# Zero rows between the queries' heads: written from a tile on chip, in two parts, instead of from a row in DRAM

## The chip, the cores and the metric

The kernel runs on one core of a Trainium2 chip. The core has a matrix engine (TensorE, PE in the profile; its weight loads are PEld), a vector engine (VectorE, DVE), a scalar engine (ScalarE, ACT), a general engine (GpSimd, POOL) and a sync engine (SyncE, SP), which here does little but issue transfers. Each engine works through its own list of instructions in order, and semaphores hold an engine until another engine, or a transfer, is done. Sixteen DMA engines move data between DRAM and the memories on chip. The metric is the device time of one execution in microseconds (us).

## The reference

The inputs are x (2048 rows of 640), and the weights of an attention with 32 heads of 20 and of a two-layer network with 1536 hidden units. Both act on 2048 rows, and a gate mixes their outputs row by row.

```python
x = A_x
g = sigmoid((x * gate_w).sum(-1, keepdims=True))
# a: attention
qkv = (x @ wqkv).reshape(B, S, 3, H, Dh).transpose(2, 0, 3, 1, 4)     # H = 32, Dh = 20
p = softmax(einsum("bhqd,bhkd->bhqk", q, k) * Dh ** -0.5)
a = einsum("bhqk,bhkd->bhqd", p, v).transpose(0, 2, 1, 3).reshape(B, S, D) @ wo
# b: network
h = einsum("bsd,df->bsf", B_x, w1) + b1
act = h * tanh(softplus(h))
b = einsum("bsf,fd->bsd", act, w2)
out = g * a + (1 - g) * b
```

## The kernel before

Heads are worked on in eight groups of four, queries in four blocks of 512. For each group and block the scores stand with the keys on the partitions: sixteen key tiles of 128 by 512 queries, for each of the four heads. A head has 20 rows, and matmuls on a quarter of the array take 32, so in the tiles QT (queries) and KT (keys) each head has 32 rows of which 12 are padding. The padding of QT must be zero.

ScalarE takes most of the exponentials: it reads two or three score tiles of 128x512 in one instruction from PSUM and writes bf16 to a ring (L1166, tile ETS). The score matmuls are L1139, the matmuls with the values L1375. VectorE takes over 118 of the 512 groups of four tiles: it makes an integer line of each tile (L1224), and shifted copies of it (L1254) which, read as float16 and weighted (VS, made by POOL at L1279), add up to the exponential. PE gives each pair of PSUM slots back when ACT has read it.

When a group is done its sums go through small transfers: VectorE copies the accumulator to OUNG (L1462), SP moves the sums to RR (L1465), VectorE inverts them (L1469), SP writes them to DRAM (SUMS<-RR, L1470) and reads them back spread over the partitions (BCT<-SUMS, L1472), and VectorE multiplies (L1432). All of this stands in the same lists as the rest.

x is needed with its columns on the partitions, in four blocks of 512 rows (XB). Block 0 is loaded as rows (L491) and transposed by PE; blocks 1 to 3 come by transposing transfers on SP (L497). Queries and keys of group 0 are made by L563 from padded weights: five matmuls for each block of x. The other groups' keys and queries are made unpadded, in denser matmuls (L625, L644 and L672), and spread by way of DRAM. For the queries, VectorE copies six heads' rows to a tile in WOQ (L680), SP writes them to the DRAM tensor QS with 32 rows for each head (QS<-WOQ, L683), and later SP reads 128 rows of QS back to QT (QT<-QS, L699). QS holds 28 heads (those of groups 1 to 7) for each of the four query blocks. The 12 rows between two heads are written once, by one transfer for each block: `clear(c)`, L593, QS<-ZEROS. Its source is one row of 512 zeros in the DRAM tensor ZEROS, repeated 336 times; ZEROS itself is written by a POOL transfer at the start. The keys take the same way through KS (L601, L617, KS<-ZEROS at L587), with ZEROS as the source of a few rows behind the last head. Every QS<-WOQ of a block waits for `q_blank[c]`, the transfer of zeros of that block.

The network's hidden units go to the tile HB (L917 adds the bias, L941 and three VectorE operations make the activation, L967 multiplies by the second weights). HB is first written at 195.73 us, apart from a second part of it which VectorE's lines use.

The order of all this is written by a planner when the program is built. It goes step by step, one ScalarE exponential to each step, keeps a modelled time for each engine, and at each step chooses from the open tasks (each with a due step) by a table of some sixty numbers: costs, margins and due steps. `later(step, fn)` puts an action at a fixed step. A new number changes the order wherever a choice was close; no number changes what is computed. At the end the last group is normalized on VectorE alone (L1447 to L1455), the output matmuls (L991) follow, and VectorE mixes their results with the network's (L997) into HB, from where they go out (L1023). A second plan, for inputs beyond a bound, stands behind a branch and is not run.

Of the kernel before, what the change touches and what calls it, by code (L numbers as in the profile page):

```python
# [21 lines left out]
H = 32  # L22
DH = 20
NG = 8
HG = 4
# [3 lines left out]
NC = 4  # L29
CW = 512  # L30
# [26 lines left out]
WIDE = 0.60  # L57
# [3 lines left out]
BLOCK = 0.43  # L61
STEP = 1.1
SLACK = 0.191
LATER = 0.79
THIRD = 0.425
CALLED = 0.978
ROWED = 3
SPARED = 0
KEPT = 8
NEED = 5  # L70
BEFORE = 4
FREE = 0.242
RISK = {"pe": 0.1, "act": 0.3, "dve": 0.5, "pool": 1.2, "sp": 1.2}
AHEAD = 17
BEHIND = 23.3
MORE = 5.902
PATIENCE = 5.499
CATCH_UP = 497.751
BUSY = 0.437
CROWD = 1.459  # L80
MARGIN = 0.679
EAGER = 121
LOAD = 1.134
MISH = 1.7
GROUP = 1.526
LAST = 0
# [1 line left out]
XSLACK = 0.468  # L88
BROAD = 1.13
FMIN = 0.109  # L90
VMIN = 12.188
ROOM = 1.319
TURN = 1
MORE_MM = 0.005
XBANKS = 2
# [1 line left out]
BEND = -0.18501488  # L97
QUART = (-1.86851238, -11.55859586, -2.86851238)
LEAD = 0.0214693053
END = 61  # L100
SHIFT = 1.385
LAG = 343
WINDOW = 2.785
CALM = 10
PACKED = 17
Q_AT = 120
# [129 lines left out]
def bass_gated_mix__softmax_full_mha__dense_activation_mish__prompt_kernel(  # L236
# [34 lines left out]
    HB = sb("HB", [P, 2, NFC, HW], BF16)  # L271
# [18 lines left out]
    QS = nc.dram_tensor("QS", [NC, 32 * (H - HG), CW], BF16, kind="Internal")  # L290
# [69 lines left out]
    def attention(pl, fast):  # L360
# [54 lines left out]
        def later(step, fn):  # L415
            at.setdefault(step, []).append(fn)
# [60 lines left out]
        b1f = []  # L477
# [3 lines left out]
        if fast:  # L481
# [13 lines left out]
            def load_x(c):  # L495
                xt_load[c] = [pl.add(
                    "sp", lambda e: e.dma_start_transpose(xt(c), x_ap[c * CW:(c + 1) * CW, :]), (), f"xt{c}", cost=4.5)]  # L497
# [14 lines left out]
            blank = early[0:NG, 4 * D + P:5 * D + P]  # L512
            m_blank = pl.add("dve", lambda e: e.memset(blank, 0.0), cost=0.25)
            m_mxs = pl.add("dve", lambda e: e.memset(MXS[:, :], 0.0))
            m_bias = pl.add("dve", lambda e: e.memset(MXR[:, 3:4], BEND))

            for i in range(10):
                pl.add("pe", lambda e: e.matmul(
                    PS[:, 5, :], RING[:, 0, 0:P], RING[:, 0, :], start=True, stop=True),
                    [m_zero] if i == 0 else [], cost=2 * PASS)  # L520
            load_x(1)
            load_x(2)

            def wbulk(name, dst, src):
# [32 lines left out]
            def kq_task(k, g, c, due, forced=True):  # L557
# [28 lines left out]
            none = ZEROS.ap()[:, 0:CW]  # L586
            k_blank = [pl.add("sp", lambda e, c=c: e.dma_start(  # L587
                KS.ap()[c, D:D + 12, :], none.to_broadcast([12, CW])), [zeros], "kz", cost=0.5) for c in range(NC)]

            def clear(c):  # L590

                to = QS.ap()[c, :, :].rearrange("(h r) t -> h r t", r=32)[:, DH:32, :]
                return pl.add("sp", lambda e: e.dma_start(to, bass.AP(  # L593
                    tensor=none.tensor, offset=none.offset, ap=[[0, H - HG], [0, 32 - DH], [1, CW]])), [zeros], f"qz{c}", cost=0.5, bulk=0.5)

            q_blank = [clear(c) for c in range(NC)]

            def shelve(name, c, rows, src, ev, n, i=0):

# [220 lines left out]
            guarded = []  # L820
# [78 lines left out]
            def h_task(hc, k, due):  # L899
# [11 lines left out]
                def finish(bank, last):  # L911
                    x_read[c].append(last)
                    w1_last[n1] = last
                    if n1 + 2 < FIRST or FIRST <= n1 < 6 * NHC - 2:
                        load_w1(n1 + 2)
                    bias = B1F[:, 2 * k:2 * k + 2].unsqueeze(2).to_broadcast([P, 2, HW])
                    ev = dve(lambda e: e.tensor_tensor(  # L917
                        hb, PS[:, bank, :].rearrange("p (i t) -> p i t", i=2), bias, ALU.add),
                        [last, *b1f, *guarded, *b_read.get(hc - 2, []), *(line_free[("h", 0)] if hc == 1 else ())], WIDE)
                    if k % 2:  # L920
                        both = HB[:, part, 2 * k - 2:2 * k + 2, :]
                        acts.append((ev, lambda: mish(ev, both, hc, k)))
                    return ev
# [556 lines left out]
        if fast:  # L1480
# [35 lines left out]
            tasks.extend(gram_task(n, SQ + SQ_STEP * n) for n in range(8))  # L1516
            tasks.extend(h_task(hc, k, H_AT + int(H_STEP * (6 * hc + k))) for hc in range(2) for k in range(6))
            tasks.sort(key=lambda t: t.due)
            later(H_AT - 90, lambda: (load_w1(0), load_w1(1)))
            rest = []  # L1520

# [157 lines left out]
        while True:  # L1679
# [50 lines left out]
            while owed > 0:  # L1730
                t = pick(limit)
# [182 lines left out]
```

## Time and profile before

| | |
|---|---|
| median of 3 runs | 781.88 us (781.61 to 783.07) |
| the profiled execution | 784.62 us |
| its span, from the first to the last instruction | 782.8 us |
| mean granted TensorE clock | 0.989 |
| busy: PE / DVE / ACT / POOL | 747.7 / 684.8 / 752.6 / 149.9 us |
| transfers of zeros to QS | 4, of 336 KB each, issued from 24.93 us on |

Times in the profile count from the start of the span. In a row of the timeline stand the start, the time it lasts, the engine (SPq is SP's issuing of transfers), the line, the operation with output <- input, the count, and in brackets the idle time ahead of it with what ended it. In a row of a group stand the count, the busy time and the mean ns of one, and then the idle time of the engine just before. In a row of the chain stand the start, the time and the work. In a row of stretches there are the busy times of PE, PEld, DVE, ACT and POOL with the number of instructions, then PE's granted clock, DMA's busy time and the GB/s that the DMA engines moved. "DMA to landing" counts from the issue. In a row of waits stand the total, the number of waits and the longest.

### The profile page before, as it was taken

Reading aid. Unit: us, or ns where it says so; the run is one execution under the profiler, and the core shown is the slowest. Engines: PE = TensorE matmul, PEld = TensorE weight load, DVE = VectorE, ACT = ScalarE, POOL = GpSimd, SP = SyncE. Lnnn points to the kernel's source line nnn. Section 1 sums busy time; section 2 is a strip of 40 time slices with the busy share of each in tenths; the row PEclk is TensorE's granted clock in tenths of the full one; section 3 lists DMA queues with packets and bytes.
Section 4 is the critical chain, followed back from the end, with each engine's and each line's share of the span. In section 5 each row is a group of like instructions: output and inputs, shape, how many; then the busy total and the mean of one; then the engine's idle time right before and its main releaser. Section 6 shows DMA issues by size and latency. Waiting matters only on the chain.

```text
span 782.8 us, 17174 instructions
## 1 busy us (share of the span) xinstructions
PE 747.7 (96%) x7176; PEld 273.9 (35%) x7176; DVE 684.8 (87%) x1108; ACT 752.6 (96%) x797; POOL 149.9 (19%) x258
## 2 busy tenths in 40 slices
PE   8969999999999999989999999999999999999996
PEld 3323334333332343223333333333333333333332
DVE  3558998999998899977798989998999999999786
ACT  5959999999999999999999999999999999999995
POOL 3203115102232013212211111311112121203200
PEclk9979999999999999999999999999999999999998
DMA  9541321021223430361111122201222211100001
GB/s 229 77 74 53 94 73 33 15 75 47 71 72 102 119 93 24 82 172 42 50 56 49 52 65 66 66 23 34 59 71 59 70 52 56 46 20 20 27 14 46
DMA packets 77804, 49.89 MB, mean 64 GB/s; under 512 B 21232, under 2 KB 73704, under 8 KB 77672
## 3 DMA queue, kind: packets, MB, share of 16 engines
q1 hardware_dynamic: 75352, 48.24, 23.2%
q8 instruction: 59, 0.97, 0.6%
q10 hardware_dynamic: 2256, 0.47, 0.3%
q0 software_dynamic: 112, 0.01, 0.1%
q14 instruction: 25, 0.20, 0.1%
HBM read 39.01 MB, written 8.90 MB: 61 GB/s over the span
## 4 chain that ended last, share of the span: by engine, by line
ACT 69%; PE 20%; DMA 6%; DVE 4%; issue 0%; SPq 0%
ACT ETS L1166 66%; PE PS L1139 7%; PE PS L1375 6%; ACT REG L941 2%; DMA W2R<-in_B_w_dram 2%; PE PS L625 2%; DMA QS<-WOQ 2%; PE PS L672 1%; PE PS L789 1%; PE PS L907 1%; DMA SUMS<-RR 1%; PE PS L830 1%; PE PS L762 1%; DMA BCT<-SUMS 1%; ACT W2R L941 1%; DMA LN<-in_A_x_dram 1%
## 5 line engine op out<-in xcount | busy, mean ns | idle before, releaser
L1166 ACT ACTIVATE ETS<-PS 128x1024 bf16<-128x1024 f32 (+1 forms) x766 | 729.1, 1134 | 14.1 <-PE PS L1139 12.6
L1139 PE MATMUL PS<-QT,KT 32*128 32x512 bf16 (+1 forms) x2118 | 300.2, 379 | 19.0 <-ACT ETS L1166 16.0
L1224 DVE TENSOR_SCALAR LN<-PS 128x512 int16<-128x512 f32 x364 | 245.1, 683 | 25.4 <-PE PS L1139 23.1
L1279 POOL TENSOR_SCALAR VS<-V_all 128x84 bf16<-128x84 bf16 x244 | 142.6, 584 | 589.3 <-PE PS L1375 396.5
L1139 PEld LDWEIGHTS PS<-QT,KT 32*128 32x128 bf16 x2118 | 74.3, 91 | 242.5 <-ACT ETS L1166 218.9
L1375 PE MATMUL PS<-ETS,V_all 128*21 128x512 bf16 (+1 forms) x1624 | 150.0, 377 | 0.3 <-DVE V_all L770 0.3
L1254 DVE TENSOR_SCALAR LN<-LN 128x2048 int16<-128x2048 int16 x163 | 111.0, 687 | 12.2 <-PE PS L1375 11.7
L967 PE MATMUL PS<-W2R,HB 128*128 128x320 bf16 x384 | 74.0, 302 | 0.5 <-DMA W2R<-in_B_w_dram 0.5
L1375 PE MATMUL PS<-LN,VS 128*21 128x512 f16 (+1 forms) x768 | 70.5, 377 | 0.0
L907 PE MATMUL PS<-XB,REG 128*128 128x256 bf16 x360 | 58.1, 275 | 0.3 <-DVE LN L1224 0.2
L1375 PEld LDWEIGHTS PS<-ETS,V_all 128*21 128x21 bf16 x1624 | 38.6, 91 | 52.8 <-issue 36.7
L991 PE MATMUL PS<-WOQ,QT 128*128 128x320 bf16 x256 | 50.9, 303 | 0.9 <-DVE QT L1455 0.9
L967 PEld LDWEIGHTS PS<-W2R,HB 128*128 128x128 bf16 x384 | 29.9, 97 | 34.8 <-issue 25.1
L1224 DVE TENSOR_SCALAR REG<-PS 128x512 int16<-128x512 f32 x52 | 34.6, 678 | 6.1 <-PE PS L1139 6.0
L907 PEld LDWEIGHTS PS<-XB,REG 128*128 128x128 bf16 x360 | 28.8, 97 | 26.3 <-issue 24.0
L1375 PE MATMUL PS<-LN,V_all 128*21 128x512 f16 (+1 forms) x380 | 35.6, 373 | 0.0
L917 DVE TENSOR_TENSOR HB<-PS,B1F 128x512 bf16<-128x512 f32 x48 | 32.6, 680 | 1.5 <-PE PS L907 1.3
L672 PE MATMUL PS<-XB,WOQ 128*120 128x512 bf16 (+1 forms) x100 | 31.4, 399 | 0.3 <-DVE WOQ L680 0.3
L991 PEld LDWEIGHTS PS<-WOQ,QT 128*128 128x128 bf16 x256 | 19.7, 97 | 25.5 <-issue 17.6
L1375 PEld LDWEIGHTS PS<-LN,VS 128*21 128x21 bf16 x768 | 17.4, 89 | 27.7 <-issue 18.8
L1462 DVE COPY OUNG<-PS 128x512 f32<-128x512 f32 x31 | 21.3, 686 | 5.6 <-PE PS L1375 5.4
L789 PE MATMUL PS<-REG,XB 128*128 128x160 bf16 (+1 forms) x240 | 25.3, 234 | 0.0
(128 smaller groups left out, 553.6 us busy)
## 6 DMA issues: line engine op xcount, KB each, us to landing
REG<-in_B_w_dram SPq DMA_DIRECT2D x36, 320.0 KB, 3.2
BCT<-SUMS SPq DMA_DIRECT2D x31, 256.0 KB
W2R<-in_B_w_dram SPq DMA_DIRECT2D x12, 320.0 KB, 4.0
QT<-QS SPq DMA_DIRECT2D x28, 128.0 KB, 2.3
KT<-KS SPq DMA_DIRECT2D x28, 128.0 KB
KS<-LN SPq DMA_DIRECT2D x16, 128.0 KB, 3.4
QS<-WOQ SPq DMA_DIRECT2D x16, 120.0 KB
W2R<-in_B_w_dram SPq DMA_DIRECT2D x1, 1920.0 KB, 13.8
```

The costliest lines, as they stand in the source:

```text
L672: return lambda e, bank: e.matmul(PS[0:m, bank, :], WQ[:, f, base:base + m], xt(c)[:, f, :], start=(f == 0), stop=(f == NFT - 1))
L789: return lambda e, bank: e.matmul(PS[:, bank, i * n:(i + 1) * n], xt(t // 4)[:, f, t % 4 * P:(t % 4 + 1) * P], WV[:, f, g * HD:g * HD + n] ...
L907: return lambda e, bank: e.matmul(PS[:, bank, i * HW:(i + 1) * HW], w1b(n1)[:, f, i * P:(i + 1) * P], xt(c)[:, f, cols], start=(f == 0), s ...
L917: ev = dve(lambda e: e.tensor_tensor(hb, PS[:, bank, :].rearrange("p (i t) -> p i t", i=2), bias, ALU.add), [last, *b1f, *guarded, *b_read ...
L967: return lambda e, bank: e.matmul(PS[:, bank, 0:HALF], HB[:, hc % 2, f, t * P:(t + 1) * P], W2[:, f, half * HALF:(half + 1) * HALF], start ...
L991: return lambda e, bank: e.matmul(PS[:, bank, 0:HALF], otn(c, g)[:, t * P:(t + 1) * P], WOG[:, g, half * HALF:(half + 1) * HALF], start=(g ...
L1139: op = pl.add("pe", lambda e, to=to, g=real(g), tile=tile, j=j, cols=cols, c=c, of_q=of_q: e.matmul(to[:, cols], KT[32 * j:32 * j + 32, g, ...
L1166: e_op[s] = pl.add("act", lambda e: e.activation(RING[:, p:p + n, :], scores(s)[:, 0:n, :], AF.Exp, scale=SCALE), [s_op[s], *(pv_slot[b] f ...
L1224: bank_free[bank] = x_ops[bank] = tile["op"] = dve(lambda e: e.tensor_scalar(dst, PS[:, bank, :], SCALE * ULPS, BASE, ALU.mult, ALU.add), ...
L1254: op = pl.add("dve", lambda e: e.tensor_scalar(to, src, SHADES[n] - SHADES[held], None, ALU.add), [made, *deps], cost=SHADE)
L1279: weighted[(c, g, k)] = n, [pl.add("pool", lambda e, i=i, n=n, src=src: e.tensor_scalar(VS[:, n, i, :, :], src, WEIGHTS[i + 1], None, ALU. ...
L1375: lasts[n] = pl.add("pe", lambda e, v=v, j=j, src=src[:, cols], of_q=of_q, begin=begin, end=end: e.matmul(PS[32 * j:32 * j + EW, ACC, of_q ...
```

## The change

The zeros' source becomes a part of HB: 28 partitions with 512 zeros each, which VectorE sets near the start (`none_q`). Each of the 28 partitions is read twelve times for the twelve rows of its head. The transfers of blocks 0 and 1 are issued between the transposing loads of x's blocks 1 and 2; those of blocks 2 and 3 go out at fixed steps, 80 and 100. They no longer wait for ZEROS but for the memset. The first writes of HB by the network wait for all four. Ten of the planner's numbers are set anew, of which two are shown.

```diff
-LATER = 0.79
+LATER = 1.264
...
-END = 61
+END = 65
...
             m_mxs = pl.add("dve", lambda e: e.memset(MXS[:, :], 0.0))
+            none_q = HB[0:H - HG, 0, 0:2, :].rearrange("p f t -> p (f t)")
+            m_none = pl.add("dve", lambda e: e.memset(none_q, 0.0), cost=0.3)
             m_bias = pl.add("dve", lambda e: e.memset(MXR[:, 3:4], BEND))
...
             load_x(1)
+            q_blank = {}
+
+            def clear(c):
+
+                to = QS.ap()[c, :, :].rearrange("(h r) t -> h r t", r=32)[:, DH:32, :]
+                q_blank[c] = pl.add("sp", lambda e: e.dma_start(
+                    to, none_q.unsqueeze(1).to_broadcast([H - HG, 32 - DH, CW])), [m_none], f"qz{c}", cost=0.8, bulk=2.5)
+
+            clear(0)
+            clear(1)
             load_x(2)
...
-            def clear(c):
-
-                to = QS.ap()[c, :, :].rearrange("(h r) t -> h r t", r=32)[:, DH:32, :]
-                return pl.add("sp", lambda e: e.dma_start(to, bass.AP(
-                    tensor=none.tensor, offset=none.offset, ap=[[0, H - HG], [0, 32 - DH], [1, CW]])), [zeros], f"qz{c}", cost=0.5, bulk=0.5)
-
-            q_blank = [clear(c) for c in range(NC)]
...
-                        [last, *b1f, *guarded, *b_read.get(hc - 2, []), *(line_free[("h", 0)] if hc == 1 else ())], WIDE)
+                        [last, *b1f, *guarded, *b_read.get(hc - 2, q_blank.values()), *(line_free[("h", 0)] if hc == 1 else ())], WIDE)
...
+            later(Q_AT - 40, lambda: clear(2))
+            later(Q_AT - 20, lambda: clear(3))
```

Lines behind the change move by 4 to 12 numbers. On SP, the start of the program before (LN are x's first rows, XB its transposed blocks, REG and WOQ the weights):

```order
L491 DMA LN<-in_A_x_dram 128x2x640 x2
L497 DMA_TRANSPOSE XB<-in_A_x_dram 128x5x512 x2
L525 DMA REG<-in_A_wqkv_dram 128x5x560
L525 DMA WOQ<-in_A_wqkv_dram 128x5x560
L525 DMA REG<-in_A_wqkv_dram 128x5x560
L497 DMA_TRANSPOSE XB<-in_A_x_dram 128x5x512
L587 DMA KS<-ZEROS 12x512 x4
L593 DMA QS<-ZEROS 28x12x512 x4
L683 DMA QS<-WOQ 6x20x512
```

and now:

```order
L491 DMA LN<-in_A_x_dram 128x2x640 x2
L497 DMA_TRANSPOSE XB<-in_A_x_dram 128x5x512
L529 DMA QS<-HB 28x12x512 x2
L497 DMA_TRANSPOSE XB<-in_A_x_dram 128x5x512
L537 DMA REG<-in_A_wqkv_dram 128x5x560
L537 DMA WOQ<-in_A_wqkv_dram 128x5x560
L537 DMA REG<-in_A_wqkv_dram 128x5x560
L497 DMA_TRANSPOSE XB<-in_A_x_dram 128x5x512
L599 DMA KS<-ZEROS 12x512 x4
L687 DMA QS<-WOQ 6x20x512
```

Two of the four transfers have moved past two loads of x, the three weight loads and the four small KS<-ZEROS; none is left ahead of the first QS<-WOQ. The third stands further down on SP, now, among the reads of keys (KT<-KS) of the second pass:

```order
L1469 DMA RR<-OUNG 128x1x16
L605 DMA KS<-LN 128x512
L621 DMA KT<-KS 128x1x512 x2
L529 DMA QS<-HB 28x12x512
L621 DMA KT<-KS 128x1x512 x2
L1474 DMA SUMS<-RR 128x16
L1476 DMA BCT<-SUMS 128x1x512
```

where before four KT<-KS stood together, directly ahead of SUMS<-RR. On DVE the multiplication that waits for this BCT (L1432) stood before in this place:

```order
L1224 TENSOR_SCALAR HB<-PS 128x512 x2
L1254 TENSOR_SCALAR LN<-LN 128x2048
L1432 TENSOR_TENSOR QT<-OUNG,BCT 128x512
L1224 TENSOR_SCALAR HB<-PS 128x512
L680 CAST WOQ<-PS 128x512
L1224 TENSOR_SCALAR LN<-PS 128x512 x3
```

and now:

```order
L1228 TENSOR_SCALAR HB<-PS 128x512 x2
L1258 TENSOR_SCALAR LN<-LN 128x2048
L1228 TENSOR_SCALAR HB<-PS 128x512
L684 CAST WOQ<-PS 128x512
L1228 TENSOR_SCALAR LN<-PS 128x512
L1436 TENSOR_TENSOR QT<-OUNG,BCT 128x512
L1228 TENSOR_SCALAR LN<-PS 128x512 x2
```

Three operations have moved ahead of it. At the end of DVE's list, before (W2R and HB are the mixes' outputs):

```order
L997 SCALAR_TENSOR_TENSOR HB<-PS,GATE,W2R 128x320
L1254 TENSOR_SCALAR LN<-LN 128x2048
L997 SCALAR_TENSOR_TENSOR HB<-PS,GATE,W2R 128x320 x3
L1449 STREAM_TRANSPOSE BCT<-PS 128x256
L1450 RECIPROCAL RR<-BCT 128x8
L1451 STREAM_TRANSPOSE BCT<-RR 128x256
L1455 TENSOR_TENSOR QT<-PS,BCT 128x256
L997 SCALAR_TENSOR_TENSOR HB<-PS,GATE,W2R 128x320 x3
```

and now:

```order
L1258 TENSOR_SCALAR LN<-LN 128x2048 x2
L1001 SCALAR_TENSOR_TENSOR W2R<-PS,GATE,XB 128x320 x2
L1453 STREAM_TRANSPOSE BCT<-PS 128x256
L1454 RECIPROCAL RR<-BCT 128x8
L1455 STREAM_TRANSPOSE BCT<-RR 128x256
L1459 TENSOR_TENSOR QT<-PS,BCT 128x256
L1001 SCALAR_TENSOR_TENSOR W2R<-PS,GATE,XB 128x320
L1001 SCALAR_TENSOR_TENSOR HB<-PS,GATE,W2R 128x320 x7
```

Five of the mixes have moved behind the last normalization. On PE, fourteen output matmuls (L995) stand in one piece between the last attention matmuls and the final eight, where before there was none. Over the whole list ACT has 740 exponentials of 1024 columns and 32 of 1536, where it had 722 and 44; the number of VectorE's lines is the same.

More of the change, by code (lines that the diff above doesn't have):

```diff
@@ L69 @@
 KEPT = 8
-NEED = 5
+NEED = 4
 BEFORE = 4
-FREE = 0.242
+FREE = 0.278
 RISK = {"pe": 0.1, "act": 0.3, "dve": 0.5, "pool": 1.2, "sp": 1.2}
-AHEAD = 17
+AHEAD = 18
 BEHIND = 23.3
@@ L79 @@
 BUSY = 0.437
-CROWD = 1.459
+CROWD = 1.561
 MARGIN = 0.679
 EAGER = 121
-LOAD = 1.134
+LOAD = 0.794
 MISH = 1.7
@@ L90 @@
 FMIN = 0.109
-VMIN = 12.188
-ROOM = 1.319
+VMIN = 11.335
+ROOM = 0.923
 TURN = 1
@@ L99 @@
 LEAD = 0.0214693053
-END = 61
+END = 65
 SHIFT = 1.385
 LAG = 343
-WINDOW = 2.785
+WINDOW = 2.367
 CALM = 10
```

## The prediction

> **What bounds the kernel now.** I read the page first: the engines' busy shares, the chain that ended last, and the groups of instructions.
>
> ```profile
> PE 747.7 (96%) x7176; PEld 273.9 (35%) x7176; DVE 684.8 (87%) x1108; ACT 752.6 (96%) x797; POOL 149.9 (19%) x258
> ACT 69%; PE 20%; DMA 6%; DVE 4%; issue 0%; SPq 0%
> L1166 ACT ACTIVATE ETS<-PS 128x1024 bf16<-128x1024 f32 (+1 forms) x766 | 729.1, 1134 | 14.1 <-PE PS L1139 12.6
> ```
>
> ScalarE's exponentials (L1166) are 729.1 of the 782.8 us and 69% of the chain. They wait only 14.1 us in all, 12.6 of it for score matmuls (L1139). So the end moves with three things: how much ACT has to do, where ACT stands idle, and what follows its last exponential. The second question is where those 14.1 us are. The waits of ACT between 46 and 62 us give the first row below; the timelines of ACT, PE and DVE show the hole itself.
>
> ```profile
> ACT ETS L1166 <- PE PS L1139: 9.8, 6, 6.6
> 53.64 1.02 ACT L1166 ACTIVATE ETS<-PS 128x1024 bf16<-128x1024 f32 x1 [6.56 <-PE PS L1139]
> 52.50 0.56 PE L762 MATMUL PS<-REG,XB 128*128 128x80 bf16 x6 [6.32 <-DVE HB L1224]
> 51.56 0.25 DVE L1469 RECIPROCAL RR<-RR 128x16 f32<-128x16 f32 x1 [6.88 <-DMA RR<-OUNG]
> ```
>
> 9.8 of the 14.1 us lie in one place, and the largest piece, 6.56, is a queue of waits: ACT for PE, PE for DVE, DVE for the little transfer RR<-OUNG, which carries the softmax sums. That transfer is quick, so I ask what it stood behind: SP's timeline, the chain between 28 and 60 us, and, for comparison, the same pair of transfers in a quiet stretch.
>
> ```profile
> 24.93 5.70 SPq L593 DMA_DIRECT2D QS<-ZEROS  x4
> 36.24 0.73 SPq L683 DMA_DIRECT2D QS<-WOQ  x1
> 49.22 0.34 SPq L699 DMA_DIRECT2D QT<-QS  x1
> 49.60 0.60 SPq L1465 DMA_DIRECT2D RR<-OUNG  x1
> ...
> 36.24 12.97 DMA QS<-WOQ
> 49.60 1.93 DMA RR<-OUNG
> ...
> 186.66 0.77 SPq L683 DMA_DIRECT2D QS<-WOQ  x1
> 189.52 0.33 SPq L699 DMA_DIRECT2D QT<-QS  x1
> ```
>
> The first transfer of query rows (QS<-WOQ) needs 12.97 us; in the quiet stretch its reader follows 2.86 us after it. It went out behind the four transfers of zeros, QS<-ZEROS. SP then sits at QT<-QS until 49.22, and RR<-OUNG is next on SP. The stretches of time say how slowly the zeros move, and what the hole does to TensorE's clock (the column before the last two).
>
> ```profile
> 16.00:20.00 4.00, 4.00 (x42) 1.65 (x40) 1.18 (x2) 4.00 (x5) 0.20 (x1) 1.00 1.50 352
> 26.00:36.00 10.00, 9.92 (x92) 3.50 (x91) 6.14 (x10) 10.00 (x12) 3.01 (x8) 1.00 0.46 64
> 36.00:48.00 12.00, 10.18 (x87) 2.58 (x79) 8.68 (x15) 11.08 (x13) 0.00 (x0) 1.00 0.70 74
> ...
> 46.00:48.00 2.00, 0.18 (x1) 0.00 (x0) 0.00 (x0) 1.08 (x2) 0.00 (x0) 1.00 0.46 85
> 48.00:61.70 13.70, 9.20 (x70) 2.75 (x70) 6.89 (x12) 5.12 (x5) 1.91 (x5) 0.50 0.25 78
> ```
>
> While weights load, the DMA engines move 352 GB/s; from 26 to 48 us, with the zeros in their queues, 64 to 74. Four blocks of 336 rows of 1 KB are 1.38 MB, at some 65 GB/s 21 us: from 26 to about 47, just when QS<-WOQ is at last served. The clock is 0.50 from 48 to 61.7, and that is why five small gaps of ACT follow: 9.8 - 6.56 = 3.2 us.
>
> **The change part by part.** *The hole.*
>
> ```profile
> 40.38 0.68 DVE L1462 COPY OUNG<-PS 128x512 f32<-128x512 f32 x1
> ```
>
> The four slow transfers no longer stand ahead of the first QS<-WOQ: two are moved to the start of SP's program, two behind it, and none reads the row in DRAM. QS<-WOQ should land in about 2.9 us, near 40; RR<-OUNG then goes out when its data are there (41.1 by this row), lands 1.93 later, and the reciprocal, which DVE reached at 44.7 (51.56 - 6.88), finds it. What is late next: nothing that I find, since DVE's next matmul inputs come at once after it. PE does not stop, so the clock stays and the five gaps go too: -9.8 us. The bounds are -6.56 (the gaps stay) and -9.8.
>
> *The start.* Two issues now stand between the transposing loads of x's blocks 1 and 2. Behind them come block 2, three weight loads and block 3.
>
> ```profile
> 1.74 8.53 SPq L497 DMA_TRANSPOSE XB<-in_A_x_dram  x2
> 12.08 9.67 SPq L497 DMA_TRANSPOSE XB<-in_A_x_dram  x1
> DMA to landing us min/median/max: 11.6/11.6/11.6
> 18.53 0.38 PE L563 MATMUL PS<-XB,REG 128*128 128x512 bf16 x1
> 23.87 0.38 PE L563 MATMUL PS<-XB,REG 128*128 128x512 bf16 x1
> 24.22 0.09 PEld L1139 LDWEIGHTS PS<-QT,KT 32*128 32x128 bf16 x2 [0.28 <-ACT ETS L1166]
> L593 SPq DMA_DIRECT2D QS<-ZEROS x4: 750/776/3267, 24.9 to 27.4; - x4
> ```
>
> Block 3 is issued at 12.08 and lands 11.6 later (the third row is of that issue alone), at 23.7. Its first use is the key matmul at 23.87 (block 2's is the one at 18.53; block 2 was out of SP by 10.3, so it has time to spare). So whatever is put ahead of block 3 delays it, and PE, which works in order, then stops ahead of the scores at 24.22. Those had 0.28 us in hand, so ACT loses the delay less about 0.4. The delay: SP issues, 2 x 0.776 = 1.55, are the lower end if the queues have room; the data, 2 x 0.344 MB, take 2.0 us at 352 GB/s and 10.6 at 65. A write from the chip is in no way tied to the one DRAM row that all old zeros were read from, so I take the fast side, 1.8 us: 1.4 us of ACT. Ends: 0 (the queues had gaps) and 10.2.
>
> Here the Trainium skill speaks against the change: in "SBUF — State Buffer", section "Door 1: The DMA port swizzle", a transfer's rate goes by the ports that its partitions reach, 27.2 GB/s each. By that table partitions 0 to 27 reach seven ports, 190 GB/s, an estimate of 3.6 us for the two blocks; the loss would be 3.2 us and the sum 1.8 higher. No row of this trace shows a wide write from 28 partitions.
>
> *The memset* that makes the zeros stands on DVE ahead of its 3.36 us of waiting for the first transposes (first row below): nothing. *The later two writes.* One goes out among the four KT<-KS, ahead of the sums' way back, near 100 us.
>
> ```profile
> 6.49 2.10 DVE L711 CAST XB<-PS 128x512 bf16<-128x512 f32 x3 [3.36 <-PE PS L726]
> ...
> 100.70 6.04 DMA SUMS<-RR
> 112.18 0.69 DVE L1432 TENSOR_TENSOR QT<-OUNG,BCT 128x512 bf16<-128x512 f32 x1 [0.90 <-DMA BCT<-SUMS]
> 195.73 0.68 DVE L917 TENSOR_TENSOR HB<-PS,B1F 128x512 bf16<-128x512 f32 x1
> ```
>
> The sums' transfer already took 6.04 us there and DVE waited 0.90 for its end. One more block adds 0.78 of issue and 1.0 us of data at 352 GB/s, 1.8 together; but the new order lets DVE do three more operations of 0.6 to 0.7 us ahead of L1432. I put it at nothing, with ends -0.4 and +5 (5.3 us of data at 65 GB/s, less what DVE does meanwhile). That the first bias adds into HB (L917) now wait for all four writes costs nothing: the first is at 195.73, some 80 us behind the last write's place.
>
> *ACT's work.* Twelve exponentials of 1536 columns become eighteen of 1024; the columns are the same, and so are the 118 tiles that DVE takes over.
>
> ```profile
> L1166 ACT ACTIVATE ETS<-PS 128x1024 bf16<-128x1024 f32 x722 | 680.1, 1107 | 14.1 <-PE PS L1139 12.6 <-PE PS L1375 1.4
> L1166 ACT ACTIVATE ETS<-PS 128x1536 bf16<-128x1536 f32 x44 | 69.2, 1584 | 0.0
> ```
>
> 512 columns are 1584 - 1107 = 477 ns, so an instruction carries 153 ns of its own; six more are at most 0.9 us. Successive ones overlap (722 x 1107 is 799, busy 680), so I take 0.4, ends 0 and 0.9.
>
> *The tail.*
>
> ```profile
> 775.08 0.71 PE L991 MATMUL PS<-WOQ,QT 128*128 128x320 bf16 x4
> 776.17 0.42 DVE L1455 TENSOR_TENSOR QT<-PS,BCT 128x256 bf16<-128x256 f32 x1
> 777.14 1.47 DVE L997 SCALAR_TENSOR_TENSOR HB<-PS,GATE,W2R 128x320 bf16<-128x320 f32 x3 [0.54 <-PE PS L991]
> ```
>
> Before, only three of DVE's final mixes (L997) come after the last normalization (L1455); in the new order eight do, and PE has fourteen output matmuls left behind its last attention matmul. Five more mixes at 0.46 (1.47 for three, overlapping) are 2.3 us, less the 0.54 that DVE waited, less some 0.3 because fewer attention matmuls are left when ACT ends: about +1.5, ends 0.5 and 2.3.
>
> *The rest of the order* changes from about 125 us on, by retuned numbers. The gaps of ACT outside the hole are 14.1 - 9.8 = 4.3 us; I have no row for the new ones and take the same, ends -3 and +4.
>
> *Sum:* -9.8 + 1.4 + 0 + 0.4 + 1.5 = -6.5 us. The profiled execution, 784.62 with its span of 782.8, would become about 778.1 and 776.3. It is 2.7 above the median of the runs, 781.88, which would become **775.4**.
>
> **Rivals.**
> 1. *Writes from the chip are as slow as those from DRAM* (the destination, not the source, is the limit). Two blocks take 10.6 us at the start; ACT loses 10.2, and TensorE's clock falls as it did in the hole, 3.2 more; the block near 100 us adds 3.5. -9.8 + 10.2 + 3.2 + 3.5 + 1.9 = +9.0: 790.9, slower. It decides from a delay of block 3 of some 5.1 us on (4.7 + 3.2 + 1.9 undo 9.8). Against it: QS<-WOQ writes the same tensor and is through in under 2.9 us.
> 2. *The hole stays*, since RR<-OUNG stands behind something else on SP: 781.88 + 1.4 + 0.4 + 1.5 = 785.2. For it: SP is one queue, and two more waits precede that row. Against it: the chain names QS<-WOQ alone.
> 3. *Half the rate, and half the clock.* At 176 GB/s the two blocks take 3.9 us and ACT loses 3.5; PE's wait then halves the clock, 3.2 more: 781.88 - 9.8 + 6.7 + 1.9 = 780.7. For it: in the hole the clock was down some 2 us after PE stopped at 46.2 (52.50 - 6.32). The Trainium skill, "TensorE: Matmul & The Clock Gate", Part 1, has it fall after an idle window of about 3.4 us that runs freely; by that rule a wait of two or three us would mostly not do it, though the hole's fall came sooner.
> 4. *The new order has new holes*, or the block near 100 us opens one: +4, 779.4.
> 5. *The new order is better*, gaps of 3 us gone and the start cheap: -4, 771.4.
>
> **How the numbers follow.** Forecast 0.64 (772.5 to 778.5); rival 1 0.06, rival 2 0.04, rival 3 0.08, rival 4 0.08, rival 5 0.10. The time is the forecast's. The range, 770.0 to 780.5, takes in rivals 4 and 5 and half of 3 and leaves out 1 and 2. A run of this kernel tells 0.2%, 1.6 us. Slower: rivals 1 and 2, 0.10. Same: half of rival 3 and a little of 4, 0.04. Faster: the rest, 0.86.
>
> **What would show it.** Right: no wait of L1469's heir for RR<-OUNG, ACT without a gap from about 48 to 62, the clock 1.00 there; PE waiting 1 to 3 us for block 3 near 24; eight mixes after the last normalization. Wrong: QS<-HB at some 65 GB/s, a clock of 0.50 after 24 us, or ACT's gaps elsewhere well over 4.3 us.

## The result, and the profile after

The changed kernel takes **787.44 us** (median of 13 runs, 783.89 to 793.28); the kernel before, on the same chip, 782.12. The ratio is 1.0074, 95% interval 1.0049 to 1.0098: 0.7% slower, a small change but clear of the noise, where the forecast was 775.4 and faster. The runs of the changed kernel spread with the TensorE clock that they were granted (0.974 in the one of 793.28, 0.985 in that of 783.89). The profiled execution took 786.72 us, span 784.9, clock 0.982; its page gives:

```profile
PE 752.8 (96%) x7166; PEld 275.3 (35%) x7192; DVE 683.7 (87%) x1109; ACT 754.7 (96%) x803; POOL 155.0 (20%) x258
L1170 ACT ACTIVATE ETS<-PS 128x1024 bf16<-128x1024 f32 (+1 forms) x772 | 730.5, 1110 | 12.7 <-PE PS L1143 12.2
```

ACT's exponentials waited 14.1 us before and wait 12.7 now, almost as long, but elsewhere. The first place to look is SP, in its timeline from 6 to 53 us:

```profile
6.89 1.03 SPq L529 DMA_DIRECT2D QS<-HB  x2
7.97 6.06 SPq L497 DMA_TRANSPOSE XB<-in_A_x_dram  x1
...
15.84 10.97 SPq L497 DMA_TRANSPOSE XB<-in_A_x_dram  x1
...
47.41 0.76 SPq L687 DMA_DIRECT2D QS<-WOQ  x1
...
51.48 0.42 SPq L703 DMA_DIRECT2D QT<-QS  x1
52.26 0.61 SPq L1469 DMA_DIRECT2D RR<-OUNG  x1
```

and then the reciprocal that ended the old queue of waits, in DVE's timeline:

```profile
55.75 0.24 DVE L1473 RECIPROCAL RR<-RR 128x16 f32<-128x16 f32 x1
```

From QS<-WOQ to QT<-QS are 4.07 us here, 12.98 before, and the reciprocal has no bracket: it waited for nothing. The old hole is gone. The new one is seen in ACT's timeline from 19 us on:

```profile
21.67 1.02 ACT L1170 ACTIVATE ETS<-PS 128x1024 bf16<-128x1024 f32 x1 [2.56 <-PE PS L1143]
...
44.15 18.61 ACT L1170 ACTIVATE ETS<-PS 128x1024 bf16<-128x1024 f32 x20 [0.31 <-PE PS L1143]
```

in ACT's waits from 16 to 24 us, then from 24 to 45 (us in total, times, longest):

```profile
ACT ETS L1170 <- PE PS L1143: 3.2, 2, 2.6
ACT ETS L1170 <- PE PS L1143: 7.1, 15, 0.7
```

and in PE's timeline at the first gap:

```profile
20.49 0.61 PE L575 MATMUL PS<-XB,REG 128*128 128x512 bf16 x1 [2.26 <-DMA XB<-in_A_x_dram]
```

One gap of 2.56 us, then fifteen of 0.3 to 0.7 after each exponential up to 44 us: 2.56 + 7.1 = 9.7 us (a gap of 0.60 stands in both rows of waits). PE came to the keys of x's **block 2** at 18.23 and waited 2.26 for the load. The three transposing loads on SP, from issue to landing, after:

```profile
DMA to landing us min/median/max: 8.7/12.5/12.9
```

and before:

```profile
DMA to landing us min/median/max: 7.6/8.6/11.6
```

The stretches of time after:

```profile
16.00:19.00 3.00, 2.23 (x30) 1.14 (x28) 1.12 (x2) 3.00 (x4) 0.00 (x0) 1.00 1.24 66
19.00:44.00 25.00, 22.49 (x120) 6.41 (x123) 5.29 (x10) 15.47 (x16) 4.41 (x11) 0.52 0.43 110
44.00:62.00 18.00, 17.54 (x174) 5.53 (x175) 17.10 (x29) 17.84 (x20) 0.00 (x0) 1.00 0.16 46
```

and the first of them before:

```profile
16.00:19.00 3.00, 3.00 (x35) 1.36 (x33) 0.96 (x2) 3.00 (x4) 0.20 (x1) 1.00 1.07 389
```

Block 2 is issued at 7.97 and lands 12.5 later, at 20.5; before, its issue lasted from 6.78 to 10.27 and it landed 7.6 after its start, at 14.4. Block 3 lands 12.9 after 15.84, at 28.7 instead of 23.7. From 16 to 19 us, where the loads moved 389 GB/s before, they move 66. And the clock is 0.52 from 19 to 44 us, which is where the fifteen gaps come from: 7.1 us, against 2.6 for the wait itself (run 3 tries this). From 44 to 62, where the old hole was, it is 1.00.

The tail, in the timelines of ACT, PE and DVE after:

```profile
779.04 0.53 ACT L1785 ACTIVATE LN<-PS,GATE 128x320 f32<-128x320 f32 x1 [5.18 <-PE PS L995]
776.59 1.39 PE L995 MATMUL PS<-WOQ,QT 128*128 128x320 bf16 x6 [0.82 <-DVE W2R L1001]
779.17 1.47 DVE L1001 SCALAR_TENSOR_TENSOR HB<-PS,GATE,W2R 128x320 bf16<-128x320 f32 x3 [0.81 <-PE PS L995]
```

and of ACT before:

```profile
777.00 0.53 ACT L1779 ACTIVATE LN<-PS,GATE 128x320 f32<-128x320 f32 x1 [2.82 <-PE PS L991]
```

ACT waits 5.18 for the matmuls of its last mix instead of 2.82, 2.4 more: PE waits for DVE to free its banks, and DVE for PE.

Of the two spans: -9.8 (old hole) + 9.7 (new hole) + 2.1 (ACT's busy time) + 2.4 (tail) - 1.3 (the other waits of ACT's exponentials: 14.1 - 9.8 = 4.3, now 12.7 - 9.7 = 3.0) is +3.1. Three waits of ACT's other work make -1.1: for the network's activation (L941, 1.0 before and 0.3 now), for the first transposes (L710, 4.7 and 4.2) and for the first keys (L710, 1.5 and 1.6). That is +2.0 in all; the spans differ by 2.1.

### The profile page after: what moved, and what is told of

It is laid out like the page before. It is cut to its first block, busy times and chain, and to the rows that moved or that the text cites. A ratio compares the mean times of both kernels' runs of the same rounds, so it can differ in the third digit from the quotient of the medians.

```text
span 784.9 us, 17199 instructions
## 1 busy us (share of the span) xinstructions
PE 752.8 (96%) x7166; PEld 275.3 (35%) x7192; DVE 683.7 (87%) x1109; ACT 754.7 (96%) x803; POOL 155.0 (20%) x258
## 4 chain that ended last, share of the span: by engine, by line
ACT 69%; PE 22%; DVE 5%; DMA 3%; issue 0%; SPq 0%; ACTq 0%
ACT ETS L1170 66%; PE PS L1143 7%; PE PS L1379 6%; ACT REG L945 2%; DMA XB<-in_A_x_dram 2%; DVE LN L1228 1%; PE PS L793 1%; PE PS L676 1%; DMA RR<-OUNG 1%; PE PS L911 1%; PE PS L629 1%; PE PS L575 1%; DVE LN L1258 1%; PE PS L766 1%; PE PS L520 1%; ACT W2R L945 1%
## 5 line engine op out<-in xcount | busy, mean ns | idle before, releaser
L1170 ACT ACTIVATE ETS<-PS 128x1024 bf16<-128x1024 f32 (+1 forms) x772 | 730.5, 1110 | 12.7 <-PE PS L1143 12.2
L1143 PE MATMUL PS<-QT,KT 32*128 32x512 bf16 (+1 forms) x2134 | 307.5, 381 | 16.7 <-ACT ETS L1170 13.2
L1228 DVE TENSOR_SCALAR LN<-PS 128x512 int16<-128x512 f32 x372 | 249.4, 681 | 26.6 <-PE PS L1143 24.8
L1283 POOL TENSOR_SCALAR VS<-V_all 128x84 bf16<-128x84 bf16 x244 | 147.7, 605 | 578.9 <-PE PS L1379 399.7
L1143 PEld LDWEIGHTS PS<-QT,KT 32*128 32x128 bf16 x2134 | 76.0, 91 | 244.9 <-ACT ETS L1170 208.3
L1379 PE MATMUL PS<-ETS,V_all 128*21 128x512 bf16 (+1 forms) x1624 | 151.2, 380 | 0.3 <-DVE V_all L774 0.3
L1379 PE MATMUL PS<-LN,VS 128*21 128x512 f16 (+1 forms) x764 | 70.3, 377 | 0.5 <-DVE LN L1258 0.5
L1379 PEld LDWEIGHTS PS<-ETS,V_all 128*21 128x21 bf16 x1624 | 38.5, 91 | 50.4 <-issue 35.1
L995 PE MATMUL PS<-WOQ,QT 128*128 128x320 bf16 x256 | 49.3, 302 | 1.3 <-DVE W2R L1001 0.8
L1379 PE MATMUL PS<-LN,V_all 128*21 128x512 f16 (+1 forms) x388 | 36.4, 373 | 0.0
L995 PEld LDWEIGHTS PS<-WOQ,QT 128*128 128x128 bf16 x256 | 19.8, 97 | 24.8 <-issue 17.2
L1379 PEld LDWEIGHTS PS<-LN,VS 128*21 128x21 bf16 x764 | 17.4, 89 | 30.5 <-issue 17.6
```

The costliest lines, as they stand in the source:

```text
L995: return lambda e, bank: e.matmul(PS[:, bank, 0:HALF], otn(c, g)[:, t * P:(t + 1) * P], WOG[:, g, half * HALF:(half + 1) * HALF], start=(g ...
L1143: op = pl.add("pe", lambda e, to=to, g=real(g), tile=tile, j=j, cols=cols, c=c, of_q=of_q: e.matmul(to[:, cols], KT[32 * j:32 * j + 32, g, ...
L1170: e_op[s] = pl.add("act", lambda e: e.activation(RING[:, p:p + n, :], scores(s)[:, 0:n, :], AF.Exp, scale=SCALE), [s_op[s], *(pv_slot[b] f ...
L1228: bank_free[bank] = x_ops[bank] = tile["op"] = dve(lambda e: e.tensor_scalar(dst, PS[:, bank, :], SCALE * ULPS, BASE, ALU.mult, ALU.add), ...
L1283: weighted[(c, g, k)] = n, [pl.add("pool", lambda e, i=i, n=n, src=src: e.tensor_scalar(VS[:, n, i, :, :], src, WEIGHTS[i + 1], None, ALU. ...
L1379: lasts[n] = pl.add("pe", lambda e, v=v, j=j, src=src[:, cols], of_q=of_q, begin=begin, end=end: e.matmul(PS[32 * j:32 * j + EW, ACC, of_q ...
```

## The experiments

Theory A: the change removed the old hole by reading another source, and dug a new one by its place, two writes ahead of block 2; the rest is small. "Behind" below means issued right after the load of block 3.

**1. The place.** The two early writes go behind block 3; nothing else changes, and PE's, DVE's and ACT's lists are the same.

```diff
-            clear(0)
-            clear(1)
             load_x(2)
...
             load_x(3)
+            clear(0)
+            clear(1)
```

> The first two writes of zeros (blocks 0 and 1) are issued behind the load of x's block 3 instead of ahead of block 2's; everything else as in the changed kernel, the order on PE, DVE and ACT too. Theory A (the two writes hold up x's blocks 2 and 3, PE stops, its clock halves, and ACT loses 9.7 us between 19 and 44): ACT runs without a gap from 13 to 62, the clock is 1.00 there, and the time is 787.4 - 9.7, about 777.5 us. Theory B (the retuned order costs the time): 785 or more. Theory C (a transfer of zeros opens a hole at the first QS<-WOQ wherever it stands): a hole of ACT of some 6 us moves back to 46 us, and the time is about 787.

**774.53 us** (773.55 to 777.33), ratio to the kernel before 0.9916 (0.9889 to 0.9942). ACT's timeline from 15 us:

```profile
15.25 9.39 ACT L1170 ACTIVATE ETS<-PS 128x1024 bf16<-128x1024 f32 x10
25.12 37.84 ACT L1170 ACTIVATE ETS<-PS 128x1024 bf16<-128x1024 f32 x41 [0.47 <-PE PS L1143]
```

and the stretch in which the two writes move nearly alone:

```profile
24.00:28.00 4.00, 3.48 (x26) 1.22 (x28) 0.61 (x3) 3.53 (x5) 3.22 (x8) 1.00 0.80 160
```

51 exponentials with one gap of 0.47: neither hole is there. The place alone cost 12.9 us (787.44 - 774.53), 3 more than theory A had: besides the waits of its exponentials (12.7 to 2.5), ACT's busy time falls too (754.7 to 752.4). The writes run at 160 GB/s, not at the 352 that the forecast took. That 774.5 lies within 1 us of the forecast of 775.4 confirms nothing: the forecast was for the writes at their early place and counted 1.4 us for it, and its tail was too short.

**2. The source's width.** Each of 112 partitions, instead of 28, holds zeros and is read three times instead of twelve.

```diff
-            none_q = HB[0:H - HG, 0, 0:2, :]...
+            none_q = HB[0:4 * (H - HG), 0, 0:2, :]...
...
-                    to, none_q.unsqueeze(1).to_broadcast([H - HG, 32 - DH, CW])), ...
+                    to, none_q.unsqueeze(1).to_broadcast([4 * (H - HG), (32 - DH) // 4, CW])), ...
```

> The zeros are set on 112 partitions instead of 28, and each partition is read three times instead of twelve; place, bytes and rows written are those of the changed kernel. Theory A1 (the 28 partitions set the rate of the write): the two writes take some 2 us instead of 4.2, x's block 2 lands near 18.3 instead of 20.4, PE waits little for it or not at all, the clock stays or falls for block 3 only: 779 to 783 us. Theory A2 (the DRAM side or the issue sets the rate): as the changed kernel, 787 us.

**789.85** (787.21 to 791.34), no better. Block 2's load needs 14.1 us from issue to landing, and the two issues take 1.86 us instead of 1.03; SP's timeline, that landing, and ACT's timeline at its first gap, 5.43:

```profile
7.24 1.86 SPq L529 DMA_DIRECT2D QS<-HB  x2
DMA to landing us min/median/max: 14.1/14.1/14.1
24.48 1.02 ACT L1170 ACTIVATE ETS<-PS 128x1024 bf16<-128x1024 f32 x1 [5.43 <-PE PS L1143]
```

So block 2 does not land earlier from a wider source. The writes themselves do move faster: these are the DMA engines from 10 to 12 us in the changed kernel, and then in run 2.

```profile
DMA packets 430, 0.38 MB, mean 188 GB/s; under 512 B 79, under 2 KB 430, under 8 KB 430
...
DMA packets 634, 0.53 MB, mean 267 GB/s; under 512 B 144, under 2 KB 634, under 8 KB 634
```

The theory that the width sets the rate of the writes was right in its direction, then; what it expected of block 2 was not, so the delay is more than the time that the writes take. The Trainium skill, "SBUF — State Buffer", section "Door 1: The DMA port swizzle", has a rate go by the ports that the partitions reach, by its table an estimate of 190 GB/s for these 28; the 160 GB/s of run 1 lie near it, and 112 partitions moved more, which agrees in direction. Whether the ports set the 160 no run tries apart.

**3. The clock.** Ten matmuls that nobody reads stand ahead of the keys of blocks 2 and 3, so that PE is not idle while it waits.

```diff
             if task.done == 0:
+                for i in range(task.warm):
+                    pl.add("pe", lambda e: e.matmul(
+                        PS[:, bank, :], KT[:, 0, 0:P], KT[:, 0, 0:CW], start=True, stop=True), ...
...
                             tasks.append(kq_task(1, g, c, due - 3))
+                            tasks[-1].warm = 10 * (c > 1)
```

> Ten matmuls of 512 columns whose result is never read stand on PE ahead of the keys of x's blocks 2 and 3, so that PE is at work while it waits for them; 2.2 us each at full clock. Theory D (of the 9.7 us that ACT loses, 2.6 are the wait and 7.1 the halved clock): the clock stays at 1.00, ACT loses 2.5 to 3 for each of the two blocks, 5 to 6 in all, and the time is 783 us. Rival (the waits alone cost it, since block 3 is late too): as the changed kernel or slower, 787 to 790 us.

**780.23** (779.48 to 782.23), ratio 0.9977 (0.9963 to 0.999). ACT's timeline:

```profile
21.78 5.66 ACT L1174 ACTIVATE ETS<-PS 128x1024 bf16<-128x1024 f32 x6 [2.57 <-PE PS L1147]
...
30.75 1.99 ACT L1174 ACTIVATE ETS<-PS 128x1024 bf16<-128x1024 f32 x2 [3.31 <-PE PS L1147]
```

The first wait is the same, 2.57, but no trail of small gaps follows it. The wait for block 3 shows now too (3.31), which the slowed kernel had hidden; after it the clock is at 0.50 once more, but only for 3.41 us (31.78 to 35.19). By the medians, of the 12.9 us that the place cost, 787.44 - 780.23 = 7.2 were the halved clock and 780.23 - 774.53 = 5.7 the waits. The two profiled executions, 786.72 and 781.91, lie 4.8 apart.

**4. The ten numbers.** Run 4 is the changed kernel with the old numbers, run 5 the kernel before with the new ones.

```diff
-LATER = 1.264
+LATER = 0.79
...
```

and, in the kernel before:

```diff
-LATER = 0.79
+LATER = 1.264
...
```

> The changed kernel with the ten numbers of the planner as before: only the writes of zeros are changed. Theory A: the start loses its 9.7 us as in the changed kernel, the tail is shorter by some 2.4 us, the gaps of the middle are 4.3 instead of 2.2: about 787 us. Theory B (the retuned order costs it): faster than before by 5 us or more, 777 us.

> The kernel before, with only the ten new numbers of the planner: the four transfers of zeros read the one DRAM row at their old place. Theory A: the hole between 46 and 62 us stays (9.8 us), and the numbers by themselves, made for another plan, cost something as the old ones did in the changed kernel: 784 to 800. Rival: the new numbers are the better ones by themselves (the gaps in the middle fell from 4.3 to 2.2 us): 779 to 781.

**813.87** (813.26 to 818.38) and **794.15** (792.37 to 795.15; ratio to before 1.0153). The waits of ACT in run 4:

```profile
ACT ETS L1170 <- PE PS L1143: 18.8, 31, 2.1
ACT ETS L1170 <- PE PS L1379: 10.7, 9, 2.4
ACT LN L1785 <- PE PS L995: 9.2, 1, 9.2
```

and ACT's timeline in run 5:

```profile
53.02 1.02 ACT L1166 ACTIVATE ETS<-PS 128x1024 bf16<-128x1024 f32 x1 [5.84 <-PE PS L1139]
```

The new numbers make the kernel before 12 us slower, and the old ones the changed kernel 26; run 4 has waits for the value matmuls (L1379) and a tail of 9.2 that neither kernel has. Theory A of run 4 had 787 and missed this. The old hole stays with the new numbers (5.84 is its first gap), so the numbers did not remove it.

**5. How much ahead of block 2.** Run 6 leaves one write there and puts the other behind; run 7 puts both behind and two small transfers (28 rows, 28 KB each, to an unused part of W2R) in their place.

```diff
             clear(0)
-            clear(1)
             load_x(2)
...
             load_x(3)
+            clear(1)
```

and in run 7:

```diff
-            clear(0)
-            clear(1)
+            shams[:] = [pl.add("sp", lambda e, n=n: e.dma_start(
+                W2R[32 * n:32 * n + H - HG, 0:CW].rearrange("p (r t) -> p r t", t=CW),
+                none_q.unsqueeze(1)), [m_none], ...) for n in range(2)]
             load_x(2)
...
             load_x(3)
+            clear(0)
+            clear(1)
```

> The changed kernel with only the first block of zeros (0.34 MB) ahead of x's block 2; the second goes out behind x's block 3. The lists of PE, VectorE and ScalarE are those of the changed kernel. Theory A (what is ahead of block 2 delays it by the time that it occupies the queues, 4.2 us for two writes): half the bytes, 2.1 us of data and 0.5 us of issue, so block 2 lands near 17.4 to 17.9, about when PE comes to it (18.2), and block 3 near 26, some 2 us late. ScalarE loses 2 to 3 us there, plus up to 3 if the clock halves: 777 to 780, forecast 778. Theory P (the place is what costs: a write between two transposing loads makes the queues change over, whatever its size): block 2 near 20 as in the changed kernel, 785 to 788.

> The kernel with the first two writes behind x's block 3 (774.5), plus two small transfers at the place where the changed kernel has its writes: one row for each of the 28 partitions, 28 KB each, to an unused part of W2R. Theory A (bytes ahead of block 2 are what delays it): 0.2 us of data, so block 2 lands about 1 us later than without them (two issues), near 15.5, with time to spare; no wait of PE for it; block 3 1 to 2 us late: 774.5 to 778. Theory P (a plain transfer between two transposing ones stops the queues for some us, whatever its size): block 2 near 18.5 to 20, a hole of 3 to 9 us, 779 to 787.

**783.38** (776.84 to 785.04, 10 runs; ratio 1.0006, 0.9985 to 1.0027) and **778.20** (774.67 to 784.62, 10 runs; ratio 0.9973, 0.9943 to 1.0002). Both spread with the clock: 776.84 had 0.998 and 785.04 had 0.985; 774.67 had 0.998, 784.62 had 0.986. Both profiles are of runs with a clock of 0.998 and 0.996. Block 2's issue on SP, its landing, and PE's wait for block 3 in run 6:

```profile
7.59 4.13 SPq L497 DMA_TRANSPOSE XB<-in_A_x_dram  x1
DMA to landing us min/median/max: 8.4/8.4/8.4
25.02 0.39 PE L575 MATMUL PS<-XB,REG 128*128 128x512 bf16 x1 [1.40 <-DMA XB<-in_A_x_dram]
```

and the same in run 7:

```profile
8.65 2.86 SPq L498 DMA_TRANSPOSE XB<-in_A_x_dram  x1
DMA to landing us min/median/max: 7.2/7.2/7.2
24.96 0.39 PE L579 MATMUL PS<-XB,REG 128*128 128x512 bf16 x1 [1.10 <-DMA XB<-in_A_x_dram]
```

Block 2 lands at 16.0 with one write ahead and at 15.9 with two small ones; both are in time for 18.2, and only block 3 is late, by 1.4 and 1.1. So a plain transfer between two transposing ones does not by itself stop the queues (theory P), but the bytes do not add up evenly either: against 14.4, one write of 0.34 MB costs 1.6 us, the second 4.5 more. Theory A had 17.4 to 17.9 for one. Its times for run 6, 777 to 780, and for run 7, 774.5 to 778, were near the profiled executions (776.84 and 775.96) and were missed by both medians, in run 7 by 0.2: other executions, with a lower clock, are up to 8 us longer in run 6 and 9 in run 7. That the wait for block 3 is what sometimes lowers it fits the timing but was not tried apart.

**6. What makes the writes so expensive.** Three edits of the changed kernel, with the writes left at their place: pieces of 6 KB instead of 1 KB (run 8); a destination on chip instead of DRAM, the real writes being done behind (run 9); block 3 issued ahead of the three weight loads (run 10).

```diff
-            none_q = HB[0:H - HG, 0, 0:2, :]...
+            none_q = HB[0:H - HG, 0, :, :]...
...
-                to = QS.ap()[c, :, :].rearrange("(h r) t -> h r t", r=32)[:, DH:32, :]
+                to = QS.ap()[c, :, :].rearrange("(h r) t -> h r t", r=32)[:, DH:32, :].rearrange("h (a r) t -> h a (r t)", a=2)
...
-                    to, none_q.unsqueeze(1).to_broadcast([H - HG, 32 - DH, CW])), ...
+                    to, none_q.unsqueeze(1).to_broadcast([H - HG, 2, 6 * CW])), ...
```

In run 9 the two transfers of run 7 write twelve rows each (`0:12 * CW` of W2R, from `none_q.unsqueeze(1).to_broadcast([H - HG, 32 - DH, CW])`). Run 10 is

```diff
             load_x(2)
+            load_x(3)
...
             wbulk("wv", ...)
-            load_x(3)
```

> The changed kernel with longer pieces: each of the 28 partitions holds 3072 zeros and is read twice, in place of 512 zeros read twelve times, so a block goes out in 56 pieces of 6 KB instead of 336 of 1 KB; same bytes, same places, same order. Theory S (the writes run at 165 to 188 GB/s because each piece of 1 KB has a fixed price): the two writes take about 2 us, block 2 lands near 18, ScalarE loses 2 to 4 us in place of 9.7, 778 to 782. Theory W (writing to DRAM, or reading 28 partitions, is the limit, whatever the piece): block 2 near 20.4, 787.

> The kernel with the first two writes behind x's block 3 (774.5), plus two transfers of the same size, shape and source at the place where the changed kernel has its writes, whose destination is not DRAM but an unused part of the tile W2R on chip; nobody needs them. Theory W (the DRAM side is slow): they pass in about 2 us, block 2 lands near 18, and the start loses 1 to 4 us: 776 to 779. Theory S (1 KB pieces are slow wherever they go) or a slow source: block 2 near 20.4, the hole of 9.7 us is back, 784 to 787.

> The changed kernel with x's block 3 issued ahead of the three weight loads instead of behind them; the two writes stay ahead of block 2, and the lists of PE, VectorE and ScalarE are unchanged. Read from it is when block 2 lands, not the time, since the weights come later now and are waited for. Theory X (the start of the weight loads beside block 2's last pieces is what makes these crawl, 4 of the 6 us): block 2 lands near 16.5 to 18. Theory Y (the second write itself, with no help from the weights, costs block 2 those us): 20 to 21, as in the changed kernel (20.5). The time by either: 788 to 797, since the weights land some 5 us later than in the changed kernel.

**790.01** (784.96 to 790.14), **790.59** (788.01 to 791.64) and **790.32** (one run). Block 2's landing, from its issue, in run 8:

```profile
DMA to landing us min/median/max: 13.8/13.8/13.8
```

in run 9:

```profile
DMA to landing us min/median/max: 12.9/12.9/12.9
```

and in run 10:

```profile
DMA to landing us min/median/max: 13.2/13.2/13.2
```

From issues at 8.00, 8.74 and 7.70 these are 21.8, 21.6 and 20.9. The same two writes as in the changed kernel let block 2 land at 21.0 in run 3 and at 19.4 in run 4, so these differences are within what the profiles of one kind of start spread. Neither the length of the pieces, nor the DRAM side, nor the weight loads behind are what delays block 2. The pieces that the DMA engines took in the changed kernel, from 9 to 11, 13 to 15, 15 to 17 and 17 to 19 us (a transposing load moves in pieces under 512 B):

```profile
DMA packets 618, 0.47 MB, mean 235 GB/s; under 512 B 189, under 2 KB 618, under 8 KB 618
...
DMA packets 1836, 0.46 MB, mean 232 GB/s; under 512 B 1834, under 2 KB 1836, under 8 KB 1836
DMA packets 684, 0.18 MB, mean 91 GB/s; under 512 B 652, under 2 KB 684, under 8 KB 684
DMA packets 97, 0.11 MB, mean 56 GB/s; under 512 B 11, under 2 KB 96, under 8 KB 96
```

The queue serves the writes first; block 2's small pieces begin in earnest at 13, run well for two us, then at a third of that rate, and then almost nothing moves for two us. Of the 97 pieces from 17 to 19 only 11 are small, so it is not block 2 alone that stands still there: the first pieces of the weights, which stand behind it, hardly move either. Why all this slows down after two full writes and not after one stays open.

**7. The source alone, at the old place.** Two edits of the kernel before, with its old numbers and order: run 11 reads the tile on chip, run 12 a DRAM tensor of 28 rows, each head's twelve reads from a row of its own.

```diff
-                return pl.add("sp", lambda e: e.dma_start(to, bass.AP(
-                    tensor=none.tensor, offset=none.offset, ap=[[0, H - HG], [0, 32 - DH], [1, CW]])), ...
+                return pl.add("sp", lambda e: e.dma_start(
+                    to, none_q.unsqueeze(1).to_broadcast([H - HG, 32 - DH, CW])), ...
```

and, in run 12, `OWN.ap()` for `none_q`, with

```diff
+    OWN = nc.dram_tensor("OWN", [H - HG, CW], BF16, kind="Internal")
...
+            own = pl.add("pool", lambda e: e.dma_start(OWN.ap(), none_q), [m_none], "own")
```

> The kernel before, with one thing changed: the four transfers of zeros read the tile on chip, as in the changed kernel, in place of the one row in DRAM; they stay at their old place behind x's block 3, with the old numbers and the old order. Theory A (the source was worth the whole gain, the place and the new order cost it again): no hole between 46 and 62 us, no wait for block 2, 772 to 774, as with 28 rows in DRAM (773.4). Rival: the four at once still hold QS<-WOQ (1.38 MB at 160 GB/s end near 34, two us ahead of it; if they are slower than that, up to 5 us later): 775 to 779.

> The kernel before, with one thing changed: the zeros are read from a tensor of 28 rows in DRAM, each head from a row of its own twelve times, instead of all 336 from one single row. Same place, same issues, same destination, same bytes, same order of PE, VectorE and ScalarE. Theory R (the single row in DRAM is what held the old transfers at 64 to 74 GB/s): they go at 150 GB/s or more, QS<-WOQ lands within 3 us, the hole between 46 and 62 us goes, 772 to 774. Theory D (any DRAM source is that slow, and the source on chip is what matters): 781 to 783 as before.

**773.32** (773.14 to 774.50), ratio 0.9892 (0.9876 to 0.9909), and **773.38** (772.87 to 773.77), ratio 0.9888 (0.9871 to 0.9904): these two beat every other version. ACT's timeline in run 12, and a stretch in which the four writes move:

```profile
15.39 45.36 ACT L1171 ACTIVATE ETS<-PS 128x1024 bf16<-128x1024 f32 x49
28.00:32.00 4.00, 3.84 (x38) 1.35 (x36) 2.33 (x5) 4.00 (x5) 1.12 (x3) 1.00 0.78 256
```

and the same stretch in run 11:

```profile
28.00:32.00 4.00, 4.00 (x42) 1.39 (x38) 2.40 (x5) 4.00 (x5) 1.02 (x3) 1.00 0.82 165
```

49 exponentials without a gap. Theory R of run 12 and theory A of run 11 held. The same bytes to the same place took 64 to 74 GB/s from one DRAM row, 165 from 28 partitions and 256 from 28 DRAM rows. It was the one row, not DRAM and not the place, that made the old hole.

## Why the prediction was wrong

- **The hole: right.** -9.8 forecast, 9.8 gone; the kernels that lost it without a new one gain 7.3 us with the new order (781.85 - 774.53) and, with the old, 8.4 (781.72 - 773.32) and 8.8 (782.19 - 773.38), each against the kernel before on its chip.
- **The start: this is the step that failed**, +1.4 forecast with ends 0 and 10.2, 9.7 measured. Three things in it were wrong. The text dismissed block 2 ("out of SP by 10.3, so it has time to spare") and costed block 3 alone; but block 2 stands directly behind the two issues, had landed at 14.4 for a use at 18.5, and so had 4.1 us in hand. It landed 6.1 us later than before, so that PE waited 2.26, and the sum had no charge for that. The rate was taken from the weight loads (352 GB/s, 2.0 us); alone the writes run at 160 (0.69 MB, 4.3 us), and beyond that block 2's own pieces slowed down. And a wait of 2.26 us halved the clock for 25 us, so that 2.6 us became 9.7; the sum had no term for the clock there.
- **Rival 3 had the mechanism** (half the rate, and half the clock) and a chance of 0.08, but priced the clock at the old hole's 3.2; it took 7.1. The delay of block 3 was 5.0, just under the 5.1 from which rival 1 decides, but it was block 2 that PE waited for.
- **The clock rule.** The Trainium skill, "TensorE: Matmul & The Clock Gate", Part 1, lets the clock fall after an idle window of about 3.4 us, whose borders run freely and do not follow the program, and come back after as long a busy one. The traces agree with the length of the window, but not with what has to fill it. These are stretches of the changed kernel up to the fall and up to the rise of the clock, then the wait of run 4 for block 2 and its stretch at half clock:

```profile
16.28:19.69 3.41, 1.95 (x28) 1.00 (x26) 0.84 (x2) 2.83 (x3) 0.00 (x0) 1.00 1.15 87
19.69:43.58 23.89, 22.07 (x118) 6.32 (x121) 5.11 (x9) 15.10 (x15) 4.41 (x11) 0.50 0.43 110
...
19.38 0.61 PE L575 MATMUL PS<-XB,REG 128*128 128x512 bf16 x1 [1.27 <-DMA XB<-in_A_x_dram]
...
19.42:50.14 30.72, 29.70 (x153) 7.95 (x157) 8.66 (x15) 19.66 (x20) 4.21 (x10) 0.50 0.33 68
```

  At half clock are 23.89 us here, 30.72 in run 4, 13.66 in the old hole (48.06 to 61.72) and 3.41 in run 3: 7, 9, 4 and 1 times 3.41. But in the 3.41 us ahead of the fall PE was busy for 1.95, and then the clock stayed down with PE busy for 22.07 of 23.89 us. In run 4 a wait of 1.27 us was enough, while in the profiles of runs 6 and 7 waits of 1.40 and 1.10 left the clock at 1.00. How much work within such a window keeps the clock up is not shown. If the window's border can fall into a wait and split it, that would explain why waits of the same length lower the clock in some executions and not in others; that is argued, not tried.
- **The memset and the later two writes: nothing, as forecast.** ACT's timeline after, where the third and the fourth write go out:

```profile
80.89 45.35 ACT L1170 ACTIVATE ETS<-PS 128x1024 bf16<-128x1024 f32 x49 [0.63 <-PE PS L1143]
```

  No gap stands between 80.89 and 126.24.
- **ACT: +0.4 forecast, +1.4 in L1170.** Run 1, with the same 772 exponentials and no hole, has 728.3 busy, less than the 729.1 before; so the 1.4 came with the hole (an exponential that stands alone takes 1.02, one in a row 0.94, 9.39 for ten), and the six more cost nothing that shows.
- **The tail: right in mechanism, mis-sized**, +1.5 forecast (0.5 to 2.3), 2.4 measured: the waits for PSUM banks between PE and DVE (0.82 and 0.81) were not counted. That they are the missing 0.9 is read from the trace alone.
- **The rest of the order: 0 forecast (-3 to +4), -1.3 measured.** That the numbers fit only their own program (813.87 and 794.15) was not foreseen, and plays no part in the sum.

## What to carry to other kernels

Before a transfer is put ahead of others in a queue, list every load behind it with its landing and its first use, the very next one first, and price the writes by a row of their own kind and not by the best rate on the page. A wait of two us on the matrix engine cost three times its length through the clock here, so a small delay there is to be charged with the trail that follows. A source that repeats one row of DRAM hundreds of times is worth replacing where it stands, and a change that moves it as well should be tried in both halves: here the half that changed the source was worth 8.4 to 8.8 us, and the half that changed the place lost 12.9 (with the new numbers).

## What the runs showed of the hardware that was not expected

- 336 reads of one 1 KB row of DRAM go at 64 to 74 GB/s; twelve reads of each of 28 rows at 256, of 28 partitions at 160 to 165, in both cases to the same DRAM rows.
- 0.34 MB of plain writes ahead of a transposing load delayed it by 1.6 us, 0.69 MB by 6.1 (5.0 in run 4 and 6.6 in run 3), with the destination on chip by 7.2 and with longer pieces by 7.4; two transfers of 28 KB by 1.5. Each is one profiled execution.
- A wait of PE of 2.26 us was followed by 25 us at a clock of 0.52, though PE was 90% busy, and one of 1.27 us (run 4) by 30.72 us at 0.50. The stretches measured at half clock (3.41, 13.66, 23.89 and 30.72 us) are whole multiples of 3.41 us. With waits of 1.4 and 1.1 us (the profiled executions of runs 6 and 7) the same program ran in some executions at 0.998 and in others at 0.985.
